# Three more gate pairs by seven products in an attention + GEGLU kernel on one Trainium2 core

## The chip, the core and the metric

The kernel runs on one core of one Trainium2 chip. The metric is the device time of one execution in microseconds (us), as the median of several runs. The engines of the core work side by side and meet through semaphores: TensorE (PE) multiplies, VectorE (DVE) and ScalarE (ACT) work element by element and are the ones that read PE's results out of PSUM here, GpSimd (POOL) works element by element on SBUF, and SyncE (SP) issues most DMAs. PSUM has eight banks, numbered 0 to 7, each of 128 partitions by 512 f32 numbers.

## What is computed

```python
# q, k, v: (8 batches, 8 heads, 576, 64); heads 0-3 use a plain window of 32, heads 4-7 a window of 32 with step 4
scores = scale * q @ k.T                      # masked to the window
attn   = softmax(scores) @ v
x      = attn.transpose(0, 2, 1, 3).reshape(4608, 512)
g      = x @ w_gate                           # (512, 1536)
val    = x @ w_val                            # (512, 1536)
out    = (gelu(g) * val) @ w_out              # (1536, 512) -> (4608, 512)
```

## The kernel before

**Chunks.** The 4608 tokens are worked off in nine chunks of 512 (c = 0 to 8). A chunk has a gate phase and an out phase. In the gate phase the 12 blocks nb = 0 to 11 of 128 hidden columns are made: four matmuls of 128x512 for the gate and four for the value (L623), the gelu on ACT (`g`, L1012), and the product of both on DVE into `u_all` (`u`, L1017, which reads the value from its PSUM bank). In the out phase `u_all` is multiplied by `w_out` (L805). Attention of the next batch stands between the matmuls of the out phase, in chunks 0 to 6; chunks 7 and 8 have none.

**Seven products in the out phase.** From chunk 1 on, the out phase takes a 2x2 split of `u` (two blocks of a pair j = 0 to 5, times two halves of the tokens) and of `w_out`, and makes the product with seven block products in place of eight, in the order 1, 7, 6, 4, 5, 2, 3 over two banks (`ORDER`, `products`). Product 7 needs `ux[j, 0]` of all six pairs, product 6 needs `ux[j, 2]` of all, product 3 a half of `u_all` that is written anew. These sums are DVE's: `u_sums(j, 0)` (word `kj@0`, L766), then `kj@1@n` for n pairs at once (L771), then `kj@2@n` (L773). `part_out` (word `q`) takes parts of the result out of the banks; `q0` is a snapshot on DVE in chunks 1 to 6 (L843, into `vdiag`), after product 1 and before product 6 adds to the same bank.

**Seven products in the gate phase.** For some pairs of blocks (`IN_SEVEN`; pair j holds nb = 2j and 2j + 1) the gate phase does the same with `x` and the weights. A word `fj@product@bank` issues one product: four matmuls of 128x256 (L688), gate and value side by side in one bank. The order is 1, 2, 6, 7, 5, 4, 3, over two banks A and B by turns: 1, 6, 5, 3 go to A, and 2, 7, 4 to B. After products 1, 6 and 7 ACT copies the bank to a snapshot (`quarter_out`, L702; `vdiag`, `turned` or `stage`), after 2, 5 and 4 DVE adds a snapshot to the bank (L709, into a tile `quarter`), and product 3 is copied by ACT (L707). The next product in a bank has to wait for that read. Each of the four quarters then has its gelu on ACT (L717, 256 wide) and its product on DVE (L726, which reads two SBUF tiles). The four sums of `x` that the products use are POOL's in chunks 6 to 8 (`x_sums`, L670); those of chunk 8 are written over those of chunk 7, and their word `x8` stands in chunk 7's out phase. The sums of the weights (`gate_sums`, L655, words `hj@part`) are made once: for pair 1 by DVE in chunk 2, for pair 2 by POOL in chunk 6.

**What sets the order.** Each engine runs its instructions in the order of the program. That order is written out by hand: `gate_words` and `out_words` give strings of words, and a number in them issues so many of the phase's 128x512 or 128x256 matmuls. `BLOCKS[c]` says, for the pairs by seven products, how many product words follow each half block (`slots`), which words stand behind them (`after`), and which stand at the end. `gate_banks` gives each ordinary block its two banks. Before, pair 1 is made by seven products in chunks 3 to 8, and pair 2 in chunks 7 and 8.

Of the kernel before, what the change touches and what calls it, by code (L numbers as in the profile page):

```python
# [21 lines left out]
def kernel(  # L22
# [21 lines left out]
    NCH = NT // CH  # L44
# [42 lines left out]
    stage = const.tile([P, 3840], F32, tag="stage")  # L87
# [7 lines left out]
    snap = [vdiag.bitcast(F32)[:, DM * i : DM * i + DM] for i in range(2)] + [turned[:, 0:DM]]  # L95
# [70 lines left out]
    tiles = {}  # L166
# [458 lines left out]
    def parts_of(order):  # L625
        return [(kc, i == 0, i == len(order) - 1) for i, kc in enumerate(order)]

    ONE = ((1, (1, 4)),)
    IN_PLACES = {c: ONE if c < 7 else ONE + ((2, (2, 3)),) for c in range(3, NCH)}
    IN_SEVEN = {c: [j for j, _ in IN_PLACES[c]] for c in IN_PLACES}  # L630
    sums_at = {1: 0, 2: 2 * CH, 3: 3 * CH}
    free_pool = range(6, NCH)

    def sums_of(j, s):

        return x_all[:, s, sums_at[j] : sums_at[j] + CH].rearrange("p (m k n) -> p m k n", m=2, k=2)

    def quarters(j, m):

        i = next(i for i, (_, end) in enumerate(WC) if 2 * j * P < end)  # L640
        w = (wg_t, wv_t)[m][i][:, :, 2 * j * P - WC[i][0] : 2 * j * P - WC[i][0] + 2 * P]
        return [[w[:, 2 * k : 2 * k + 2, P * n : P * n + P] for k in range(2)] for n in range(2)]

    def gate_sums(j, part):

        for m in range(2):
            (a11, a12), (a21, a22) = quarters(j, m)
            s1, s2, s3, s4 = (sums_of(j, s)[:, m] for s in range(4))
# [6 lines left out]
            (nc.vector if j == 1 else nc.gpsimd).tensor_tensor(out_, first, other, op)  # L655
# [41 lines left out]
    def quarter_out(c, j, kind, bank):  # L697

        src, kept = ps[:, bank, :], {1: 0, 6: 1, 7: 2}.get(kind)
        saved = snap if bank in (1, 4) else [stage[:, DM * i : DM * i + DM] for i in range(3)]  # L700
        if kept is not None:
            nc.scalar.copy(saved[kept], src)  # L702
            return
        n = tiles["quarters"] = tiles.get("quarters", 0) + 1
        t = nrm.tile([P, S], F32, tag=("rb", "lg", "rb", "lg", "rb")[n % 5], bufs=(3, 2, 3, 2, 3)[n % 5], name="quarter")[:, 0:DM]
        if kind == 3:
            nc.scalar.copy(t, src)  # L707
        else:
            nc.vector.tensor_tensor(t, src, saved[{2: 0, 4: 1, 5: 2}[kind]], ALU.add)  # L709
        nb, half = 2 * j + (kind in (4, 5)), int(kind in (3, 5))  # L710
        tiles.setdefault("ready", []).append((nb, half, t))
# [238 lines left out]
    def gate_banks(c, nb):  # L950

        if c == 0:
            return ((4, 5), (6, 7))[nb] if nb < 2 else ((0, 1), (2, 3))[nb % 2]
        if c in IN_SEVEN:
            if nb in (1, 11):
                return (1, 4)
            if c > 6:
                return (5, 6) if nb % 2 else (0, 7)
            return (4, 1) if nb == 9 else (0, 7)
        return ((0, 7), (1, 6) if c == 1 else (1, 4))[nb % 2]  # L960

    SEVEN = range(1, NCH)
# [1 line left out]
    def gate_list(c):  # L964
# [28 lines left out]
    def run_program(c, words, mms, banks):  # L993
# [3 lines left out]
        for word in words.split():  # L997
# [12 lines left out]
            elif kind == "g":  # L1010
                g = ffn.tile([P, CH], F16, tag="g")
                nc.scalar.activation(g, ps[:, gate_banks(c, args[0])[0], :], AF.Gelu)  # L1012
                tiles["g", args[0]] = g
            elif kind == "u":
# [47 lines left out]
    def gate_words(c):  # L1062
# [35 lines left out]
    one = (  # L1098
        [0, 1, 1, 0, 1, 1, 0, 1, 1, 1, 0, 0, 0, 0, 0],
        "||k0@0||k2@0||||k3@0|k3@1@2|U k3@2@2|U|U k4@0|k1@0|k1@1@2",  # L1100
    )
    late = "|".join(w + h for w, h in zip(one[1].split("|"), [""] * 11 + [" h2@0", " h2@1", " h2@2", " h2@3"]))
    two = (
        [0, 2, 2, 2, 2, 2, 2, 2, 0, 0, 0],
        "k0@0||||k3@0|||U|U k4@0|U k1@0 k2@0|k2@1@3",
    )
    BLOCKS = {c: (*one, "", "") for c in range(3, 6)}
    BLOCKS[6] = (one[0], late, "", "")
    BLOCKS[7] = BLOCKS[8] = (*two, "", "u11 k5@0 k5@1@3 k2@2@3 k5@2@3")

    def seven_words(c):

        pairs = IN_PLACES[c]
        orders = [[f"f{j}@{product}@{banks[n % 2]}" for n, product in enumerate((1, 2, 6, 7, 5, 4, 3))] for j, banks in pairs]
        pairs = [j for j, _ in pairs]
        groups = orders[0] if len(pairs) == 1 else [w for both in zip(*orders[:2]) for w in both]
# [12 lines left out]
    def out_words(c):

        if c == 0:
            return (
                "V1 F2 S6@4+S7@6 1 E P6 11 P7 1 M6 S4@4+S5@6 M7 1 P4 6 P5 M4 2 D6@40+D7@60 l6 l7 M5 r6 r7 6 w2@0 4 w1@0 4 "
                "w0@0 H2 N6@50+N7@20 D4@52+D5@22 X6 l5 X7 l4 r4 r5 10 N4@20+N5@40 X4 X5 2 e3@0"
            )
        if c > 6:
            return "12 q0@1 x8 12 q1@1 12 q2@1 12 q3@0 12 q4@0 12 q5@0 12 q6@1" if c < NCH - 1 else "L"
        i, j, k, l = (NHP * (c + 1) + n for n in range(NHP))
        v0, v1 = (" v0", " v1") if 2 < c < 6 else ("", "")
        late = "k1@2@2 " if c in IN_SEVEN else ""  # L1140
# [14 lines left out]
    }  # L1155
# [38 lines left out]
```

## Time and profile before

| | |
|---|---|
| median of 3 runs | 315.9 us (315.34 to 315.94) |
| the profiled execution | 316.73 us, of which span 315.0 us |
| busy in the span | DVE 227.7 us, ACT 179.5 us, POOL 104.4 us |
| granted PE clock | 1.00 |
| gate phase and out phase of chunk 7 | 252.92 to 272.93 us and 272.93 to 282.22 us |
| gate phase and out phase of chunk 8 | 282.22 to 302.14 us and from 302.14 us on |

A row of the timeline has the start, the time to the end of the last instruction, the engine, the line, the operation, what is written and read with its shape, and the count; in brackets stands idle time before it and what ended it. Matmuls are pipelined: each is shown from its issue to its modelled end, so rows overlap, and the step from one start to the next is the time that it costs PE. DVE and ACT overlap the start of one instruction with the end of the one before in the same way.

### The profile page before, as it was taken

The numbers are of one execution on the slowest core, as the hardware profiler recorded it, in microseconds if no ns is written. First come the engines' busy times: TensorE is split into PE (matmuls) and PEld (weight loads), VectorE is DVE, ScalarE is ACT, GpSimd is POOL, SyncE is SP. The second block draws the span as 40 slices with busy tenths as digits, with TensorE's granted clock in tenths as the row PEclk, the third lists the DMA queues.
The fourth block names the chain that finished last, engine by engine and source line by source line (L and its number), as shares of the span: only waits on it lengthen the run. The fifth ranks groups of instructions, "written<-read, shape, count | busy, mean of one in ns | idle before, by whom it ended". The sixth has DMA issues, their size and how long they took to land.

```text
span 315.0 us, 8745 instructions
## 1 busy us (share of the span) xinstructions
PE 308.0 (98%) x3585; PEld 193.2 (61%) x3585; DVE 227.7 (72%) x408; ACT 179.5 (57%) x295; POOL 104.4 (33%) x154
## 2 busy tenths in 40 slices
PE   7999999999999999999999999999999999999995
PEld 4854545446854486557755775568556856686674
DVE  6863656698866798698858886797568757944772
ACT  2673476535763387547754675567556765524740
POOL 8784703312367160233126031504730052300000
PEclk9999999999999999999999999999999999999999
DMA  8999998898699998889889667965200220021004
GB/s 188 186 197 206 206 198 150 241 207 194 152 281 180 198 221 157 237 202 212 184 220 251 156 180 174 230 156 146 67 0 4 69 69 0 2 99 36 0 0 135
DMA packets 110791, 47.16 MB, mean 150 GB/s; under 512 B 83616, under 2 KB 110240, under 8 KB 110752
## 3 DMA queue, kind: packets, MB, share of 16 engines
q1 hardware_dynamic: 97248, 38.29, 53.9%
q0 software_dynamic: 12944, 7.67, 19.1%
q10 hardware_dynamic: 560, 0.66, 0.8%
q8 instruction: 28, 0.46, 0.7%
q14 instruction: 11, 0.09, 0.1%
HBM read 37.75 MB, written 9.44 MB: 150 GB/s over the span
## 4 chain that ended last, share of the span: by engine, by line
PE 88%; DVE 5%; DMA 4%; POOL 1%; issue 1%; ACT 0%; DVEq 0%
PE ps L623 49%; PE ps L805 21%; PE ps L688 8%; PE ps L458 6%; PE ps L730 3%; DMA wg<-in_moe_w_gate_dram 2%; DMA xT<-in_q_dram 2%; DVE u_all L1017 1%; DVE ux L766 1%; DVE ux L771 1%; DVE P L493 1%; DVE vdiag L843 1%; DVE u_all L726 0%; POOL xT L182 0%; PE ps L378 0%
## 5 line engine op out<-in xcount | busy, mean ns | idle before, releaser
L1012 ACT ACTIVATE g<-ps 128x512 f16<-128x512 f32 x92 | 54.8, 597 | 78.8 <-PE ps L623 78.7
L1017 DVE SCALAR_TENSOR_TENSOR u_all<-g,ps 128x512 f16<-128x512 f16 x92 | 63.0, 685 | 49.9 <-PE ps L623 33.3
L623 PE MATMUL ps<-xT,wv 128*128 128x512 f16 x368 | 95.8, 379 | 0.0
L623 PE MATMUL ps<-xT,wg 128*128 128x512 f16 x368 | 95.0, 379 | 0.2
L623 PEld LDWEIGHTS <-wg 128*128 128x128 f16 x368 | 35.8, 98 | 38.7 <-DMA wg<-in_moe_w_gate_dram 0.2
L623 PEld LDWEIGHTS <-wv 128*128 128x128 f16 x368 | 36.0, 98 | 37.0 <-DMA wv<-in_moe_w_val_dram 0.4
L805 PEld LDWEIGHTS <-u_all 128*128 128x128 f16 x390 | 36.8, 98 | 7.1 <-issue 1.1
L805 PE MATMUL ps<-wx,ux 128*128 128x256 f16 x288 | 35.5, 273 | 0.6 <-DVE vdiag L843 0.5
L805 PE MATMUL ps<-wo,u_all 128*128 128x256 f16 (+1 forms) x294 | 35.2, 271 | 0.0
L254 POOL CAST v<-stage 128x1152 f16<-128x1152 f32 x11 | 13.0, 1177 | 64.4 <-DMA stage<-in_v_dram 48.2
L217 POOL CAST s<-stage 128x640 f16<-128x640 f32 x24 | 17.7, 767 | 44.5 <-DMA stage<-in_q_dram 31.1
L614 DVE TENSOR_TENSOR xT<-ps,rb 128x576 f16<-128x576 f32 x32 | 29.1, 940 | 4.7 <-PE ps L458 3.2
L488 ACT ACTIVATE P<-ps 128x832 f16<-128x832 f32 (+1 forms) x32 | 25.3, 834 | 12.1 <-PE ps L458 12.0
L805 PEld LDWEIGHTS <-ux 128*128 128x128 f16 x288 | 27.6, 98 | 4.9 <-issue 1.0
L670 POOL TENSOR_TENSOR xT<-xT 128x512 f16<-128x512 f16 x12 | 13.9, 1182 | 33.0 <-DVE xT L614 25.4
L766 DVE TENSOR_TENSOR ux<-u_all 128x512 f16<-128x512 f16 x48 | 22.4, 478 | 0.8
L585 ACT ACTIVATE lg<-ps 128x576 f32<-128x576 f32 x30 | 18.8, 656 | 6.6 <-PE ps L458 3.6
L229 POOL CAST s<-stage 128x512 f16<-128x512 f32 x24 | 16.2, 700 | 8.8 <-DMA stage<-in_q_dram 8.1
L591 ACT ACTIVATE rb<-lg 128x576 f32<-128x576 f32 x30 | 19.0, 687 | 0.1
L688 PE MATMUL ps<-xT 128*128 128x256 f16 x128 | 17.9, 273 | 0.0
L726 DVE SCALAR_TENSOR_TENSOR u_all<-g,quarter 128x256 f16<-128x256 f16 x32 | 15.8, 497 | 1.8 <-ACT g L717 1.8
L688 PEld LDWEIGHTS <-xT 128*128 128x128 f16 x128 | 12.5, 98 | 6.6
(113 smaller groups left out, 358.2 us busy)
## 6 DMA issues: line engine op xcount, KB each, us to landing
out_dram<-part SPq DMA_DIRECT2D x30, 256.0 KB, 2.8
stage<-in_v_dram SPq DMA_DIRECT2D x28, 144.0 KB, 3.5
stage<-in_q_dram SPq DMA_DIRECT2D x24, 128.0 KB, 3.5
stage<-in_k_dram SPq DMA_DIRECT2D x24, 128.0 KB, 3.0
stage<-in_q_dram SPq DMA_DIRECT2D x6, 512.0 KB, 4.9
stage<-in_k_dram SPq DMA_DIRECT2D x6, 512.0 KB, 5.5
stage<-in_v_dram SPq DMA_DIRECT2D x20, 128.0 KB, 3.4
wo<-in_moe_w_out_dram POOLq DMA_DIRECT2D x3, 512.0 KB, 15.7
```

The costliest lines, as they stand in the source:

```text
L217: nc.gpsimd.tensor_copy(s16[:, 1280 * t + 640 * g : 1280 * t + 640 * g + 640].rearrange("p (k c) -> p k c", k=5), st_of(i).rearrange("p (k ...
L458: nc.tensor.matmul(o[cols], lhs[rows], rhs[rows], start=st, stop=end, skip_group_check=True)
L488: nc.scalar.activation(pt[:, 0 : src.shape[1]], src, AF.Exp, bias=0.0, scale=scale)
L585: nc.scalar.activation(lg, psf[:, c0 : c0 + S], AF.Ln)
L591: nc.scalar.activation(rb, tiles.pop(("lg", n)), AF.Exp, scale=-1.0)
L614: nc.vector.tensor_tensor(dst, num, rb, ALU.mult)
L623: nc.tensor.matmul(ps[:, bank, :], w[:, kc, ns], xT[kc][:, tok], start=first, stop=end)
L688: nc.tensor.matmul(ps[:, bank, 2 * P * m : 2 * P * m + 2 * P], left[:, k], right[:, k], start=first and m == 0 and k == 0, stop=k == 1, sk ...
L766: nc.vector.tensor_tensor(ux[:, j, 0:2], k0, u_all[:, 2 * j : 2 * j + 2, hi], ALU.subtract)
L805: lambda o=o, s=s[:, P * p : P * p + P], t=t[:, c0:c1], st=st, end=end: nc.tensor.matmul(o, s, t, start=st, stop=end, skip_group_check=True)
L1012: nc.scalar.activation(g, ps[:, gate_banks(c, args[0])[0], :], AF.Gelu)
L1017: nc.vector.scalar_tensor_tensor(u_all[:, nb, :], tiles.pop(("g", nb)), -USCALE if c in SEVEN and nb % 2 else USCALE, val, ALU.mult, ALU.mult)
```

## The change

Chunk 6 makes pairs 1 and 2 by seven products, one pair behind the other in the banks 1 and 4. Chunks 7 and 8 make pairs 1, 2 and 3 (a, b and c in `in_turn`) on the banks 1 and 2, 6 and 3, 4 and 5. Six products stand together behind block 1, then three behind each half block. Blocks 8, 9 and 10 all use the banks 0 and 7, block 11 the banks 3 and 5. In chunks 7 and 8 product 3 is no longer copied: gelu and product read it from its bank. The sums of pair 2's weights move from POOL in chunk 6 to DVE in chunk 5; POOL makes those of pair 3 in chunk 6. In the out phases of chunks 1 to 6 the snapshot `q0` moves ahead of `k5@1`, and in chunk 6 `k3@2` covers pairs 2 and 3 late.

```diff
-    ONE = ((1, (1, 4)),)
-    IN_PLACES = {c: ONE if c < 7 else ONE + ((2, (2, 3)),) for c in range(3, NCH)}
-    IN_SEVEN = {c: [j for j, _ in IN_PLACES[c]] for c in IN_PLACES}
+    IN_PLACES = {c: {1: (1, 4)} for c in range(3, 6)}
+    IN_PLACES[6] = {1: (1, 4), 2: (4, 1)}
+    IN_PLACES[7] = IN_PLACES[8] = {1: (1, 2), 2: (6, 3), 3: (4, 5)}
+    IN_SEVEN = {c: list(IN_PLACES[c]) for c in IN_PLACES}
...
-            (nc.vector if j == 1 else nc.gpsimd).tensor_tensor(out_, first, other, op)
+            (nc.gpsimd if j == 3 else nc.vector).tensor_tensor(out_, first, other, op)
...
+        if kind == 3 and c > 6:
+            tiles.setdefault("ready", []).append((2 * j, 1, src))
+            return
...
-            if nb in (1, 11):
-                return (1, 4)
-            if c > 6:
-                return (5, 6) if nb % 2 else (0, 7)
-            return (4, 1) if nb == 9 else (0, 7)
+            if nb == 11:
+                return (1, 4) if c < 7 else (3, 5)
+            return (1, 4) if nb == 1 else (4, 1) if nb == 9 and c < 6 else (0, 7)
...
     two = (
-        [0, 2, 2, 2, 2, 2, 2, 2, 0, 0, 0],
-        "k0@0||||k3@0|||U|U k4@0|U k1@0 k2@0|k2@1@3",
+        [0, 2, 2, 2, 2, 2, 2, 1, 1, 0, 0],
+        "k0@0||||k3@0|h3@0||k1@0 k1@1@2|U k4@0|U h3@1|U h3@2 k2@0",
     )
...
+    early = ["", " h2@0", "", " h2@1", "", " h2@2", " h2@3"]
+    BLOCKS[5] = (one[0], "|".join(w + h for w, h in zip(one[1].split("|"), early + [""] * 8)), "", "")
...
-    BLOCKS[7] = BLOCKS[8] = (*two, "", "u11 k5@0 k5@1@3 k2@2@3 k5@2@3")
+    three = ([6, 3, 3, 3, 3, 3, 0], "k0@0||||k4@0|U k1@0|U")
...
+    BLOCKS[6] = (*two, "h3@3 k3@1@2", "")
+    BLOCKS[7] = BLOCKS[8] = (*three, "U k2@0 k3@0", "u11 k5@0 k3@1@4 k5@1@2 k3@2@4 k5@2@2")
+    in_turn = "a1 b1 a2 a6 b2 a7 a5 b6 c1 a4 b7 c2 a3 b5 c6 b4 c7 c5 b3 c4 c3"
...
-            f"E P{i} P{j} 1 u11 k5@0 k5@1@2 11 q0@0 M{i} M{j}{v0} {late}k5@2@2 12 q1@1 8 "
+            f"E P{i} P{j} 1 u11 k5@0 11 q0@0 k5@1@2 M{i} M{j}{v0} {late}k5@2@2 12 q1@1 8 "
```

The first place is DVE's queue at the end of chunk 3's gate phase, before the change: the last block's product, the last pair's sums, the snapshot `vdiag`, and the masks of the attention tiles `P`.

```order
L1017 SCALAR_TENSOR_TENSOR u_all<-g,ps 128x512
L766 TENSOR_TENSOR ux<-u_all 128x512
L771 TENSOR_TENSOR ux<-u_all,ux 128x2x256
L843 TENSOR_SCALAR vdiag<-ps 128x512
L493 TENSOR_TENSOR P_2480<-P_2480,two_p 128x832
```

And with the change (L847 is the snapshot, L775 the sum that stood ahead of it):

```order
L1019 SCALAR_TENSOR_TENSOR u_all<-g,ps 128x512
L770 TENSOR_TENSOR ux<-u_all 128x512
L847 TENSOR_SCALAR vdiag<-ps 128x512
L775 TENSOR_TENSOR ux<-u_all,ux 128x2x256
L493 TENSOR_TENSOR P_2480<-P_2480,two_p 128x832
```

The snapshot has moved ahead of one sum; nothing else has moved there.

The second place is ACT's queue at the start of chunk 7's gate phase, before the change: the load of the gelu table, the gelus of blocks 0 to 2, the first snapshots of pairs 1 and 2 and the gelu of block 3.

```order
L1059 ACT_TABLE_LOAD
L1012 ACTIVATE g<-ps 128x512 x3
L702 COPY vdiag<-ps 128x512
L702 COPY stage<-ps 128x512
L1012 ACTIVATE g<-ps 128x512
```

And with the change:

```order
L1061 ACT_TABLE_LOAD
L1014 ACTIVATE g<-ps 128x512 x2
L703 COPY vdiag<-ps 128x512
L703 COPY stage<-ps 128x512
L703 COPY vdiag<-ps 128x512
L721 ACTIVATE g<-quarter 128x256
```

The gelu of the third block is gone from there: the products of a pair now follow block 1 directly.

The third place is DVE's queue in the last third of chunk 7's gate phase. Before, from the last read of a bank for a quarter (L709) on: quarters' products (L726), blocks 9, 10 and 11 (L1017), and the sums `ux`.

```order
L709 TENSOR_TENSOR quarter<-ps,stage 128x512
L726 SCALAR_TENSOR_TENSOR u_all<-g,quarter 128x256 x3
L1017 SCALAR_TENSOR_TENSOR u_all<-g,ps 128x512
L726 SCALAR_TENSOR_TENSOR u_all<-g,quarter 128x256
L766 TENSOR_TENSOR ux<-u_all 128x512
L726 SCALAR_TENSOR_TENSOR u_all<-g,quarter 128x256
L766 TENSOR_TENSOR ux<-u_all 128x512 x2
L1017 SCALAR_TENSOR_TENSOR u_all<-g,ps 128x512
```

With the change, from block 9 (L1019) to block 10 (the last row), where three reads for quarters (L713) still stand:

```order
L1019 SCALAR_TENSOR_TENSOR u_all<-g,ps 128x512
L730 SCALAR_TENSOR_TENSOR u_all<-g,ps 128x256
L713 TENSOR_TENSOR quarter<-ps,stage 128x512
L730 SCALAR_TENSOR_TENSOR u_all<-g,quarter 128x256
L713 TENSOR_TENSOR quarter<-ps,stage 128x512
L770 TENSOR_TENSOR ux<-u_all 128x512
L730 SCALAR_TENSOR_TENSOR u_all<-g,quarter 128x256
L713 TENSOR_TENSOR quarter<-ps,stage 128x512
L730 SCALAR_TENSOR_TENSOR u_all<-g,quarter 128x256
L730 SCALAR_TENSOR_TENSOR u_all<-g,ps 128x256
L770 TENSOR_TENSOR ux<-u_all 128x512
L1019 SCALAR_TENSOR_TENSOR u_all<-g,ps 128x512
```

Behind these twelve rows come two more quarters' products, two sums, block 11, the last pair's first sum, and `k3@1@4`, a sum over four pairs in one instruction. Before, the reads for quarters were over when the last sums began; now they stand among them.

More of the change, by code (lines that the diff above doesn't have):

```diff
@@ L699, in quarter_out @@
         src, kept = ps[:, bank, :], {1: 0, 6: 1, 7: 2}.get(kind)
-        saved = snap if bank in (1, 4) else [stage[:, DM * i : DM * i + DM] for i in range(3)]
+        saved = snap if j == 1 else [stage[:, DM * i : DM * i + DM] for i in range(3 * j - 6, 3 * j - 3)]
         if kept is not None:
             nc.scalar.copy(saved[kept], src)
+            return
+        if kind == 3 and c > 6:
+            tiles.setdefault("ready", []).append((2 * j, 1, src))
             return
@@ L1101 @@
     )
-    late = "|".join(w + h for w, h in zip(one[1].split("|"), [""] * 11 + [" h2@0", " h2@1", " h2@2", " h2@3"]))
+    early = ["", " h2@0", "", " h2@1", "", " h2@2", " h2@3"]
     two = (
-        [0, 2, 2, 2, 2, 2, 2, 2, 0, 0, 0],
-        "k0@0||||k3@0|||U|U k4@0|U k1@0 k2@0|k2@1@3",
-    )
-    BLOCKS = {c: (*one, "", "") for c in range(3, 6)}
-    BLOCKS[6] = (one[0], late, "", "")
-    BLOCKS[7] = BLOCKS[8] = (*two, "", "u11 k5@0 k5@1@3 k2@2@3 k5@2@3")
-    def seven_words(c):
[L1113 to L1116, printed above, removed]
+        [0, 2, 2, 2, 2, 2, 2, 1, 1, 0, 0],
+        "k0@0||||k3@0|h3@0||k1@0 k1@1@2|U k4@0|U h3@1|U h3@2 k2@0",
+    )
+    three = ([6, 3, 3, 3, 3, 3, 0], "k0@0||||k4@0|U k1@0|U")
+    BLOCKS = {c: (*one, "", "") for c in range(3, 5)}
+    BLOCKS[5] = (one[0], "|".join(w + h for w, h in zip(one[1].split("|"), early + [""] * 8)), "", "")
+    BLOCKS[6] = (*two, "h3@3 k3@1@2", "")
+    BLOCKS[7] = BLOCKS[8] = (*three, "U k2@0 k3@0", "u11 k5@0 k3@1@4 k5@1@2 k3@2@4 k5@2@2")
+    in_turn = "a1 b1 a2 a6 b2 a7 a5 b6 c1 a4 b7 c2 a3 b5 c6 b4 c7 c5 b3 c4 c3"
+    def seven_words(c):
+        places = IN_PLACES[c]
+        order = (1, 2, 6, 7, 5, 4, 3)
+        turns = [(j, product) for j in places for product in order]
+        if len(places) == 3:
+            turns = [("_abc".index(w[0]), int(w[1])) for w in in_turn.split()]
+        groups = [f"f{j}@{product}@{places[j][order.index(product) % 2]}" for j, product in turns]
+        pairs = list(places)
         direct = [nb for nb in range(2, NNB - 1) if nb // 2 not in pairs]
@@ L1139, in out_words @@
         v0, v1 = (" v0", " v1") if 2 < c < 6 else ("", "")
-        late = "k1@2@2 " if c in IN_SEVEN else ""
+        late = "" if c < 3 else "k1@2@2 " if c < 6 else "k1@2@2 k3@2@2 "
         after = f"S{l + 1}@12+S{l + 2}@15" if 1 < c < 6 else ""
         return (
-            f"E P{i} P{j} 1 u11 k5@0 k5@1@2 11 q0@0 M{i} M{j}{v0} {late}k5@2@2 12 q1@1 8 "
+            f"E P{i} P{j} 1 u11 k5@0 11 q0@0 k5@1@2 M{i} M{j}{v0} {late}k5@2@2 12 q1@1 8 "
             f"S{k}@1+S{l}@4 D{i}@11+D{j}@41 P{k} P{l} 4 q2@0 M{k} M{l}{v1} 12 l{i} l{j} r{i} r{j} q3@0 "
```

## The prediction

> **What bounds the kernel now.** I read the page first (busy shares, then the chain), then the windows of chunks 7 and 8, then the timeline of the places that the change touches.
>
> ```profile
> span 315.0 us, 8745 instructions
> PE 308.0 (98%) x3585; PEld 193.2 (61%) x3585; DVE 227.7 (72%) x408; ACT 179.5 (57%) x295; POOL 104.4 (33%) x154
> PE 88%; DVE 5%; DMA 4%; POOL 1%; issue 1%; ACT 0%; DVEq 0%
> 252.92:272.93 20.01, 20.01 (x123) 11.74 (x121) 15.12 (x27) 13.29 (x26) 8.27 (x7) 1.00 0.08 26
> 282.22:302.14 19.92, 19.92 (x122) 11.73 (x120) 13.00 (x27) 11.90 (x25) 0.00 (x0) 1.00 0.08 27
> ```
>
> PE is busy 98% of the span and carries 88% of the chain. In the gate phases of chunks 7 and 8 (the windows; columns PE, PEld, DVE, ACT, POOL) it has no gap at all. So PE columns that are saved are time saved, as long as DVE, the next engine at 15.12 of 20.01 us in chunk 7, still empties banks and delivers sums in time. That is the question.
>
> **What the change saves on PE.** PE's step is read where nothing waits, in chunk 8:
>
> ```profile
> 290.01 1.04 PE L688 MATMUL ps<-xT 128*128 128x256 f16 x8
> 290.88 1.03 PE L623 MATMUL ps<-xT,wv 128*128 128x512 f16 x4
> 291.74 1.04 PE L688 MATMUL ps<-xT 128*128 128x256 f16 x8
> ```
>
> Eight matmuls of 128x256 take 0.87 us from start to start, four of 128x512 take 0.86: 0.109 and 0.216 each. A pair made the ordinary way is 16 x 0.216 = 3.46, by seven products 28 x 0.109 = 3.05. Saved are 0.40 us a pair, and three more pairs (one each in chunks 6, 7, 8) give **-1.2**.
>
> **The snapshot ahead of the second sum.** Chunk 3, then chunk 4:
>
> ```profile
> 143.23 0.76 DVE L766 TENSOR_TENSOR ux<-u_all 128x512 f16<-128x512 f16 x1
> 144.02 0.86 DVE L771 TENSOR_TENSOR ux<-u_all,ux 128x512 f16<-128x512 f16 x1
> 144.81 0.68 DVE L843 TENSOR_SCALAR vdiag<-ps 128x512 f32<-128x512 f32 x1
> 143.55 1.47 PE L805 MATMUL ps<-wx,ux 128*128 128x256 f16 x12
> 145.54 1.03 PE L805 MATMUL ps<-wx,ux 128*128 128x256 f16 x8 [0.52 <-DVE vdiag L843]
> 177.55 0.68 DVE L843 TENSOR_SCALAR vdiag<-ps 128x512 f32<-128x512 f32 x1
> 176.71 2.61 PE L805 MATMUL ps<-wx,ux 128*128 128x256 f16 x20
> ```
>
> In chunk 3 product 7 began at 143.55, so product 6 was due 12 x 0.109 later, at 144.86, and began at 145.54, 0.05 after the snapshot's end: 0.68 lost. With the sum behind it the snapshot starts at 143.9 and ends at 144.6, in time. In chunk 4 twenty matmuls end after 2.61 us where 19 steps and one whole instruction (0.38 less 0.11, as eight take 1.04) make 2.34: 0.27 lost, and gone too. The sum moved back is needed only by product 6's last two pairs, 0.9 us later. But in chunk 3 the masks behind it still have to pass POOL's casts, and PE, now earlier, meets them. Bounds 0 and -0.95; I take **-0.6**.
>
> **Start of chunk 7.** Product a1 goes to bank 1, where block 1's gate lies until its gelu has read it.
>
> ```profile
> 256.22 0.60 ACT L1012 ACTIVATE g<-ps 128x512 f16<-128x512 f32 x1 [0.60 <-PE ps L623]
> 256.45 0.38 PE L623 MATMUL ps<-xT,wg 128*128 128x512 f16 x1
> ```
>
> The second row is the first matmul behind block 1, an ordinary one in bank 0. In its place now stands a1, which must wait for 256.82 and the 0.05 seen above: 0.42 of PE standing. Then a7 wants bank 2 after DVE's add on a2, with two products (0.87) between; the add takes 0.68, the hand-overs around it 0.27 and 0.05 (rows below): 0.1. Together **+0.5** (bounds 0.4 and 0.7). In chunk 8 block 1's gate comes four matmuls earlier, and this is nothing.
>
> **End of chunk 7.** This is the large term. The instructions' steps on DVE, and what POOL's subtractions for chunk 8 do to them:
>
> ```profile
> 258.19 1.03 PE L623 MATMUL ps<-xT,wv 128*128 128x512 f16 x4
> 259.32 0.69 DVE L1017 SCALAR_TENSOR_TENSOR u_all<-g,ps 128x512 f16<-128x512 f16 x1 [1.12 <-PE ps L623]
> 259.93 0.68 DVE L709 TENSOR_TENSOR quarter<-ps,vdiag 128x512 f32<-128x512 f32 x1
> 260.53 0.68 DVE L709 TENSOR_TENSOR quarter<-ps,stage 128x512 f32<-128x512 f32 x1
> 265.38 4.98 POOL L670 TENSOR_TENSOR xT<-xT 128x512 f16<-128x512 f16 x4 [7.46 <-PE ps L688]
> 266.62 1.15 POOL L670 TENSOR_TENSOR xT<-xT 128x512 f16<-128x512 f16 x1
> 267.73 2.63 POOL L670 TENSOR_TENSOR xT<-xT 128x512 f16<-128x512 f16 x2
> 267.48 0.57 DVE L726 SCALAR_TENSOR_TENSOR u_all<-g,quarter 128x256 f16<-128x256 f16 x1
> 268.57 2.41 DVE L726 SCALAR_TENSOR_TENSOR u_all<-g,quarter 128x256 f16<-128x256 f16 x3
> 271.50 0.41 DVE L726 SCALAR_TENSOR_TENSOR u_all<-g,quarter 128x256 f16<-128x256 f16 x1
> 271.84 0.41 DVE L766 TENSOR_TENSOR ux<-u_all 128x512 f16<-128x512 f16 x1
> 272.17 0.41 DVE L726 SCALAR_TENSOR_TENSOR u_all<-g,quarter 128x256 f16<-128x256 f16 x1
> 273.78 0.55 DVE L771 TENSOR_TENSOR ux<-u_all,ux 128x768 f16<-128x768 f16 x1
> L726 DVE SCALAR_TENSOR_TENSOR u_all<-g,quarter x32: 411/419/1378, 133.2 to 300.5; 128x256 f16<-128x256 f16 x32
> ```
>
> PE's last matmul ends 0.17 after its issue (1.03 less 0.86), and DVE starts 0.10 later (259.32). An instruction that reads a bank steps by 0.60, a quarter's product or a 512-wide sum by 0.34. Those have both inputs in SBUF, and while POOL ran (265.38 to 270.36) the same product took 0.57 and then 2.41 for three, its longest 1.38 against a median of 0.42. The bank reads in the same stretch kept their 0.68. The 0.57 one ended at 268.05, 0.28 after POOL's second subtraction (until 267.77): of its 0.41 it had used 0.13. POOL in turn was held: with 1.02 of its 1.15 still to run after each DVE instruction, the last two end at 268.05 + 1.02 + 0.28 + 1.02 = 270.37, as the row has it (267.73 + 2.63). So the two take turns, each for its whole length.
>
> Now the queue. Let T be when c5, the 18th of the 21 products, has left PE's issue. Behind it PE issues blocks 10 and 11 (16 x 0.216), b3, c4, c3 (12 x 0.109), and the out phase's products 1 and 7 (24 x 0.109): product 6 is due at T + 7.4. It needs `k3@1@4`. On DVE that instruction stands behind block 9's product, which starts at T - 1.04 (its value matmuls leave PE three products, 1.31, earlier, and end and hand over 0.27 later). From there come six bank reads at 0.60 and twelve short ones at 0.34, 0.11 of waits on own results (the sum of 144.02 began 0.03 after the end it needed, where bank reads overlap by 0.08), and the sum over four pairs at 0.69 (0.55 for three pairs in the last row but one, 0.42 for two): 8.5, so T + 7.5. **Without POOL DVE arrives just in time**, 0.1 late.
>
> But POOL's four subtractions begin as c5 ends, at T + 0.2, as they began in the trace when the last product 5 had ended. Walked by the turns above: DVE's product at T + 0.51 waits for POOL's first to end (T + 1.35) and ends at T + 1.63; the sum at T + 2.15 waits for the second and ends at T + 2.93; the product at 2.85 waits for the third, until T + 4.23; the one at 4.75 for the fourth, until T + 5.53. The next instruction starts at T + 5.45, where it would stand at T + 3.07 undisturbed: 2.4 lost, and product 6 is late by **+2.5**, part of it earlier, at c3, block 11's value and product 7, which wait in the same queue. Bounds: 0.1 if POOL runs clear of it, 4.2 if each of the four turns costs a whole 1.02; the 1.46 that the before lost in its own 5 us (0.57 + 2.41 for four, against 4 x 0.34 and 0.15 of overlap) lies between. I take my walk. The before loses almost nothing here, as its last bank reads are over by then: 24 matmuls took 2.90 in chunk 7 against 2.78 in chunk 8, **-0.1** of an old wait that the new one contains.
>
> ```profile
> 274.24 2.90 PE L805 MATMUL ps<-wx,ux 128*128 128x256 f16 x24
> 303.45 2.78 PE L805 MATMUL ps<-wx,ux 128*128 128x256 f16 x24
> ```
>
> The Trainium skill ("SBUF — State Buffer", section "Who interferes with whom") speaks against the change here: a DVE instruction with two SBUF inputs and a GpSimd instruction that reads SBUF share a port pair under an exclusive lock, and the later one blocks fully. The 1.38 and the 0.28 agree. By a proportional slowdown, say the 1.46 again, the term would be 1.6 and not 2.5.
>
> **The rest.** Chunk 8 has the same queue without POOL (0.00 in its window): some 0.1, and DVE's waits for gelus, which chunk 7 hides in its backlog; bounds 0 and 0.7, I take **+0.4**. In chunk 6 DVE has about two us more (three bank reads and four short ones for two bank reads), with six products on one bank pair by turns: bounds 0 and 0.6, **+0.2**. In chunk 5 eight weight sums come to DVE,
>
> ```profile
> L655 DVE TENSOR_TENSOR xT<-wg x2: 283/284/284, 97.4 to 104.4; 128x256 f16<-128x256 f16 x2
> ```
>
> at 0.28 each, 0.20 in step, 1.6 in all, beside POOL's casts of batch 7: bounds 0 and 0.8, **+0.3**. POOL's own sums in chunk 6 are as many as before. Product 3 without its copy takes work from ACT, which has slack (13.29 of 20.01), and costs or gains nothing; its quarter's product then reads a bank, which POOL doesn't disturb, and the banks it keeps are wanted only a phase later. No DMA moves.
>
> **Sum.** -1.2 - 0.6 + 0.5 + 2.5 - 0.1 + 0.4 + 0.2 + 0.3 = **+2.0**. On the profiled execution (316.73, span 315.0) that is 318.7; the median of the runs is 0.8 lower, 315.9, so I forecast **317.9**.
>
> **Rivals.** *POOL runs clear of DVE* (not slower): if DVE's short instructions fall between POOL's, or DVE is ahead, the 2.5 shrinks to 0.1 and the sum to -0.4: 315.5. It decides at the end of chunk 7, at whether `k3@1@4` ends by T + 7.4. For it speaks that the queue fits without POOL; against it that the four subtractions take 5 us and that four two-input instructions stand in just that stretch. *PE is bound by its columns alone* (faster): every wait hidden, -1.2 - 0.95 = -2.1: 313.8. Against it stands the wait of a1, which no queue can hide. *The backlog costs more* (slower): all turns at their full price and chunks 5, 6 and 8 at their upper bounds, about +4.9: 320.8; with chunks 5, 6 and 8 alone at theirs, +3.2: 319.1.
>
> **How the numbers follow.** Forecast 0.74, from about +0.8 to +3.2, 316.7 to 319.1; POOL clear 0.12; columns alone 0.04; more 0.10. A difference of 0.2% (0.6 us) is about what a measurement of this kernel can tell from none. The POOL rival's time lies within it or just below: 0.06 faster, 0.06 same. So faster is 0.06 + 0.04 = 0.10, same 0.06, slower 0.74 + 0.10 = 0.84. The range for 8 in 10 runs from 316.0, toward the POOL rival, to 319.4, into the heavier one.
>
> **What would show it.** Right: in chunk 7 a PE wait of 0.4 on ACT's gelu ahead of the first L689 row; four POOL rows (L671) of 1.15 to 1.35 from the end of the 18th product on, with DVE rows L730 or L770 of 0.8 to 1.4 between them; PE idle on DVE in front of c3, block 11's value and the out phase's products 7 and 6, 2.5 us in all; in chunk 8 only some tenths; no wait on the snapshot L847 in chunks 3 and 4. Wrong: chunk 7's two phases no longer than 28.9 us (29.3 before, less 0.4), or DVE's L730 at 0.42 throughout.

## The result, and the profile after

The changed kernel takes 318.99 us (median of 6 runs, 318.08 to 319.57) against 316.03 of the kernel before in the runs beside it (315.34 to 317.02): a ratio of **1.0076, interval 1.0052 to 1.01**, so slower. The profiled execution took 319.11 us, its span 317.3 against 315.0.

Busy shares and the chain, from the page of the kernel after:

```profile
span 317.3 us, 8850 instructions
PE 307.6 (97%) x3621; PEld 195.9 (62%) x3621; DVE 234.4 (74%) x431; ACT 184.4 (58%) x307; POOL 104.6 (33%) x154
PE 85%; DVE 8%; POOL 2%; DMA 2%; issue 1%; ACT 0%
```

PE is busy 0.4 us less than before and the span is 2.3 us longer: DVE's share of the chain grew from 5% to 8%. The same window as in the prediction shows where, from the start of chunk 7's gate phase to that of chunk 8 (columns: length, then PE, PEld, DVE, ACT, POOL, clock, DMA share, GB/s):

```profile
252.67:284.54 31.87, 30.08 (x219) 20.56 (x217) 23.81 (x42) 16.33 (x32) 8.34 (x7) 1.00 0.10 33
```

The two phases took 29.30 us before (252.92 to 282.22), with PE busy throughout; now 31.87, with PE idle for 1.8 by its rows and for 3.0 by its steps (a row runs on to the modelled end, which covers part of a wait). The timeline of PE says what it waits for: first the masks in chunks 1 and 2, the out phase of chunk 3, a stall at 187 us, block 9 in chunk 6, then the start of chunk 7, its end, and chunk 8:

```profile
80.68 0.55 PE L458 MATMUL ps<-P,ones 64*64 64x96 f16 x22 [0.24 <-DVE P L493]
...
114.38 0.55 PE L458 MATMUL ps<-P,ones 64*64 64x96 f16 x22 [0.37 <-DVE P L493]
...
144.16 2.35 PE L809 MATMUL ps<-wx,ux 128*128 128x256 f16 x20
...
186.03 0.54 PE L458 MATMUL ps<-q 64*64 64x96 f16 x35
187.42 0.19 PE L458 MATMUL ps<-q 64*64 64x64 f16 x1 [0.85 <-issue]
...
256.62 0.38 PE L689 MATMUL ps<-xT,wg 128*128 128x256 f16 x2 [0.25 <-ACT g L1014]
...
268.09 1.03 PE L623 MATMUL ps<-xT,wg 128*128 128x512 f16 x4
...
270.42 0.60 PE L689 MATMUL ps<-xT 128*128 128x256 f16 x4 [0.43 <-DVE quarter L713]
...
273.01 1.02 PE L623 MATMUL ps<-xT,wv 128*128 128x512 f16 x4 [0.27 <-DVE quarter L713]
...
275.98 0.95 PE L809 MATMUL ps<-wx,ux 128*128 128x256 f16 x6 [0.17 <-DVE ux L770]
277.37 0.39 PE L809 MATMUL ps<-wx,ux 128*128 128x256 f16 x2 [0.45 <-DVE ux L770]
277.98 1.48 PE L809 MATMUL ps<-wx,ux 128*128 128x256 f16 x12 [0.21 <-DVE ux L775]
...
284.54 1.03 PE L623 MATMUL ps<-xT,wg 128*128 128x512 f16 x4
...
304.22 1.47 PE L809 MATMUL ps<-wo,u_all 128*128 128x256 f16 x12
```

Each bracket understates a wait by 0.17, the tail of the matmul before it. Counted from start to start, less the 0.109 or 0.216 of each matmul, the end of chunk 7 loses 0.60 ahead of c3 (270.42), 0.43 ahead of block 11's value (273.01), 0.34, 0.11 and 0.61 inside product 7, and 0.37 ahead of product 6 (277.98): **2.46 us**. In chunk 3, twenty matmuls of products 7 and 6 run in 2.35, as they should; the wait on the snapshot is gone. Chunk 8's gate phase, 284.54 to 304.22, is 19.68 long against 19.92 before.

DVE's timeline at the same place, from block 9's product on:

```profile
266.98 0.69 DVE L1019 SCALAR_TENSOR_TENSOR u_all<-g,ps 128x512 f16<-128x512 f16 x1 [0.28 <-PE ps L623]
267.58 0.41 DVE L730 SCALAR_TENSOR_TENSOR u_all<-g,ps 128x256 f16<-128x256 f16 x1
267.91 0.68 DVE L713 TENSOR_TENSOR quarter<-ps,stage 128x512 f32<-128x512 f32 x1
268.51 1.25 DVE L730 SCALAR_TENSOR_TENSOR u_all<-g,quarter 128x256 f16<-128x256 f16 x1
269.69 0.68 DVE L713 TENSOR_TENSOR quarter<-ps,stage 128x512 f32<-128x512 f32 x1
270.29 0.78 DVE L770 TENSOR_TENSOR ux<-u_all 128x512 f16<-128x512 f16 x1
270.99 1.37 DVE L730 SCALAR_TENSOR_TENSOR u_all<-g,quarter 128x256 f16<-128x256 f16 x1
272.28 0.68 DVE L713 TENSOR_TENSOR quarter<-ps,stage 128x512 f32<-128x512 f32 x1
272.88 0.77 DVE L730 SCALAR_TENSOR_TENSOR u_all<-g,quarter 128x256 f16<-128x256 f16 x1
273.58 0.41 DVE L730 SCALAR_TENSOR_TENSOR u_all<-g,ps 128x256 f16<-128x256 f16 x1
...
277.23 1.02 DVE L775 TENSOR_TENSOR ux<-u_all,ux 128x1024 f16<-128x1024 f16 x2
```

And POOL's, whose four subtractions of `x8` fill 268.33 to 273.37:

```profile
268.33 5.04 POOL L671 TENSOR_TENSOR xT<-xT 128x512 f16<-128x512 f16 x4 [10.64 <-PE ps L689]
```

Exactly the four instructions with two SBUF inputs that start in that stretch are long, 1.25, 0.78, 1.37 and 0.77 where undisturbed ones take 0.41 or 0.42; the reads of a bank between them (269.69, 272.28) keep 0.68. All products of line L730 that read a tile `quarter`, with minimum, median and maximum in ns:

```profile
L730 DVE SCALAR_TENSOR_TENSOR u_all<-g,quarter x38: 410/417/1370, 133.8 to 303.7; 128x256 f16<-128x256 f16 x38
```

The longest of the whole kernel is the one at 270.99; half of the 38 take 0.417 or less.

### The profile page after: what moved, and what is told of

Read it like the earlier page. It is cut to its first block, busy times and chain, and to the rows that moved or that the text cites. A ratio compares the mean times of both kernels' runs of the same rounds, so it can differ in the third digit from the quotient of the medians.

```text
span 317.3 us, 8850 instructions
## 1 busy us (share of the span) xinstructions
PE 307.6 (97%) x3621; PEld 195.9 (62%) x3621; DVE 234.4 (74%) x431; ACT 184.4 (58%) x307; POOL 104.6 (33%) x154
## 4 chain that ended last, share of the span: by engine, by line
PE 85%; DVE 8%; POOL 2%; DMA 2%; issue 1%; ACT 0%
PE ps L623 45%; PE ps L809 21%; PE ps L689 9%; PE ps L458 6%; PE ps L734 3%; DMA wg<-in_moe_w_gate_dram 2%; DVE u_all L730 2%; DVE u_all L1019 1%; DVE P L493 1%; DVE ux L770 1%; DVE quarter L713 1%; POOL xT L182 1%; POOL v L313 1%; DVE vdiag L847 0%; DVE ux L775 0%
## 5 line engine op out<-in xcount | busy, mean ns | idle before, releaser
L1019 DVE SCALAR_TENSOR_TENSOR u_all<-g,ps 128x512 f16<-128x512 f16 x86 | 58.7, 684 | 44.3 <-PE ps L623 29.6
L623 PE MATMUL ps<-xT,wv 128*128 128x512 f16 x344 | 89.7, 379 | 0.3 <-DVE quarter L713 0.3
L623 PE MATMUL ps<-xT,wg 128*128 128x512 f16 x344 | 88.8, 379 | 0.1
L1014 ACT ACTIVATE g<-ps 128x512 f16<-128x512 f32 x86 | 51.2, 597 | 64.3 <-PE ps L623 64.1
L623 PEld LDWEIGHTS <-wv 128*128 128x128 f16 x344 | 33.5, 98 | 35.4 <-issue 1.0
L623 PEld LDWEIGHTS <-wg 128*128 128x128 f16 x344 | 33.4, 98 | 35.5 <-DMA wg<-in_moe_w_gate_dram 0.2
L217 POOL CAST s<-stage 128x640 f16<-128x640 f32 x24 | 17.9, 776 | 42.8 <-DMA stage<-in_q_dram 30.7
L689 PE MATMUL ps<-xT 128*128 128x256 f16 x176 | 24.8, 273 | 0.4 <-DVE quarter L713 0.4
L689 PEld LDWEIGHTS <-xT 128*128 128x128 f16 x176 | 16.9, 98 | 8.1 <-issue 0.6
L770 DVE TENSOR_TENSOR ux<-u_all 128x512 f16<-128x512 f16 x48 | 20.9, 443 | 0.8
L730 DVE SCALAR_TENSOR_TENSOR u_all<-g,quarter 128x256 f16<-128x256 f16 x38 | 19.4, 510 | 0.7 <-ACT g L721 0.7
```

The source lines that it names most:

```text
L623: nc.tensor.matmul(ps[:, bank, :], w[:, kc, ns], xT[kc][:, tok], start=first, stop=end)
L689: nc.tensor.matmul(ps[:, bank, 2 * P * m : 2 * P * m + 2 * P], left[:, k], right[:, k], start=first and m == 0 and k == 0, stop=k == 1, sk ...
L730: nc.vector.scalar_tensor_tensor(dst, g, by, t[:, 2 * P : 4 * P], ALU.mult, ALU.mult)
L770: nc.vector.tensor_tensor(ux[:, j, 0:2], k0, u_all[:, 2 * j : 2 * j + 2, hi], ALU.subtract)
L1019: nc.vector.scalar_tensor_tensor(u_all[:, nb, :], tiles.pop(("g", nb)), -USCALE if c in SEVEN and nb % 2 else USCALE, val, ALU.mult, ALU.mult)
```

## The experiments

The theory: the 2.46 us at the end of chunk 7 come from POOL's four subtractions, which stop DVE's two-input instructions in turns while PE waits on DVE's queue. The rivals: DVE's queue has simply become too long there (three pairs' quarters, then a sum over four pairs at the end), or the turns are an old cost that the kernel before paid as well. A second theory, on 0.4 us, is the bank of the first product.

Each ratio is taken against the kernel before in runs beside the version's own. Its median there was 316.72 us for `x8` on DVE, its control, the swapped banks and the three edits together, and 316.38 for the other four, where it was 316.03 beside the change. So versions are compared by their ratios, not by their times.

**The `x8` subtractions on DVE.** One number takes them from POOL; DVE makes them after `k3@2@4`.

```diff
-    free_pool = range(6, NCH)
+    free_pool = range(6, NCH - 1)
```

> The changed kernel with chunk 8's four x subtractions on DVE, where they stand behind the last u sum of chunk 7, in place of POOL. Theory (POOL and DVE take turns at the end of chunk 7): PE's waits there, 2.5 us in the trace of the change (c3, block 11's value, products 7 and 6), shrink to 0.1 to 0.5, DVE's L730 products stay at 0.42, and the time falls by 2.2 to 2.6 us, to about 316.5, 1.001 to 1.003 of before. Rival (DVE simply has too much to do for three pairs): four more DVE instructions of 0.42 make it no better, 319 to 320.

Measured: 315.95 us (315.39 to 318.09, 12 runs), ratio 0.9982 (0.9961 to 1.0003), below the 1.001 to 1.003 that was expected. DVE's timeline at the same place:

```profile
267.85 0.42 DVE L730 SCALAR_TENSOR_TENSOR u_all<-g,quarter 128x256 f16<-128x256 f16 x1
268.18 0.68 DVE L713 TENSOR_TENSOR quarter<-ps,stage 128x512 f32<-128x512 f32 x1
268.78 0.42 DVE L770 TENSOR_TENSOR ux<-u_all 128x512 f16<-128x512 f16 x1
269.12 0.42 DVE L730 SCALAR_TENSOR_TENSOR u_all<-g,quarter 128x256 f16<-128x256 f16 x1
...
275.92 1.62 DVE L671 TENSOR_TENSOR xT<-xT 128x512 f16<-128x512 f16 x4
```

And PE's, from the out phase's product 1 on:

```profile
272.19 1.47 PE L809 MATMUL ps<-wo,u_all 128*128 128x256 f16 x12
273.50 2.78 PE L809 MATMUL ps<-wx,ux 128*128 128x256 f16 x24
```

All six waits are gone: the 24 matmuls of products 7 and 6 take the 2.78 us that they take undisturbed. DVE's queue up to the sum that product 6 needs is as long as in the change (the 1.62 us of subtractions stand behind it), and PE waits for nothing in it. So a queue that is too long by itself falls as a cause. The span is 314.1, 3.2 shorter; 2.46 of that are these waits, and 0.65 the stall at 187 us, which is 0.36 in this run and 1.01 in that of the change and was no part of the expectation (more on it at the end of the next section).

**The same edit on the kernel before**, as a control.

> The kernel before with chunk 8's x subtractions on DVE, as in e1: the control. Theory: POOL's subtractions cost PE 0.1 us there, since the reads of banks are over when they run, so -0.1, within 0.1% of before, although DVE's products of 0.57 to 1.38 us go. Rival (the subtractions on POOL cost a fixed price wherever they stand): -2 us, as in e1.

Measured: 315.9 us (315.49 to 318.13, 12 runs), ratio 0.9984 (0.9966 to 1.0002). The 0.11 at product 7 is gone; a gain beyond that isn't resolved. So the turns were not an old cost of this size: the subtractions ran in the kernel before too, beside instructions that nobody waited for.

**The subtractions once more, in chunk 8.** Here POOL repeats them at the same point of the last chunk, which has the same queue on DVE and no POOL work in the change. No later instruction uses what they write.

```diff
-            return "12 q0@1 x8 12 q1@1 ... 12 q6@1" if c < NCH - 1 else "L"
+            return "12 q0@1 x8 12 q1@1 ... 12 q6@1" if c < NCH - 1 else "x8 L"
```

> The changed kernel in which POOL makes chunk 8's four x subtractions once more, into the same places, as soon as chunk 8's products have read them: the suspected cost added at the end of chunk 8, where POOL had nothing to do; nothing reads the result. Theory (two-input DVE instructions and POOL's reads take turns): PE waits at the end of chunk 8 for 2.5 us more, DVE's L730 and L770 of 0.8 to 1.4 us appear there, +2.4 to +2.6 us, about 321.5. Rival (chunk 7's waits come from DVE's load, POOL is a bystander): the same 319.0.

Measured: 321.4 us (320.99 to 321.8, 4 runs), ratio 1.0147 (1.0097 to 1.0197), 0.7% above the change. PE's timeline in chunk 8:

```profile
301.19 0.60 PE L689 MATMUL ps<-xT 128*128 128x256 f16 x4 [0.43 <-DVE quarter L713]
...
303.78 1.02 PE L623 MATMUL ps<-xT,wv 128*128 128x512 f16 x4 [0.27 <-DVE quarter L713]
...
305.44 1.36 PE L809 MATMUL ps<-wo,u_all 128*128 128x256 f16 x11 [0.53 <-ACT g L1014]
307.67 2.78 PE L809 MATMUL ps<-wx,ux 128*128 128x256 f16 x24 [0.88 <-DVE u_all L1019]
```

The waits ahead of c3 and block 11's value are those of chunk 7, 0.60 and 0.43. Then come 0.69 ahead of the second matmul of product 1 and 1.04 ahead of product 7: 2.76 in all, where the change has 0.22. DVE's held instructions are those of chunk 7 again, 1.25, 0.77, 1.37 and 0.77 (at 299.28, 301.06, 301.76 and 303.65). The mechanism could be put where it was wanted, at the price of chunk 7, though the waits behind it fall on other instructions: product 7 here waits for DVE's read of block 11's value (L1019), which lies in bank 5.

**POOL busy at that point, but not reading.** Four memsets of the same four pieces in place of the repeated subtractions; no later instruction uses them.

```diff
+            elif kind == "Z":
+                for s in (1, 0, 2, 3):
+                    nc.gpsimd.memset(x_all[:, s, CH : 2 * CH], 0.0)
...
-            return "12 q0@1 x8 12 q1@1 ... 12 q6@1" if c < NCH - 1 else "L"
+            return "12 q0@1 x8 12 q1@1 ... 12 q6@1" if c < NCH - 1 else "Z L"
```

> As e5, but POOL sets the four 128x512 pieces of the x sums to zero at that point in place of subtracting: it writes SBUF and reads none; nothing reads the result. Theory (the turns are over reads): DVE keeps 0.42, no change, 319.0. Rival (any POOL instruction on SBUF blocks DVE's two-input ones): +0.5 to +2.5 us, by how long the memsets run.

Measured: 318.06 us (317.77 to 319.57, 10 runs), ratio 1.0051 (1.0027 to 1.0075), no slower than the change. POOL's timeline in chunk 8:

```profile
298.54 1.45 POOL L1045 MEMSET xT<- 128x512 f16 x3 [26.31 <-PE ps L689]
300.28 0.52 POOL L1045 MEMSET xT<- 128x512 f16 x1 [0.28 <-PE ps L689]
```

And DVE's beside it:

```profile
298.74 0.42 DVE L730 SCALAR_TENSOR_TENSOR u_all<-g,quarter 128x256 f16<-128x256 f16 x1
299.07 0.69 DVE L713 TENSOR_TENSOR quarter<-ps,stage 128x512 f32<-128x512 f32 x1
299.68 0.42 DVE L770 TENSOR_TENSOR ux<-u_all 128x512 f16<-128x512 f16 x1
```

The product at 298.74 lies wholly within the row of three memsets (298.54 to 299.99, 0.48 each) and takes its 0.42, and so does the sum at 299.68, which starts within it; PE's waits in chunk 8 stay at the 0.34 of the change. The turns are over reads of SBUF, then, not over POOL being busy or writing. One input is enough: where POOL casts, in the change for instance in the row of two casts (L217) from 135.96 to 137.54, DVE's sum at 136.99 (L775, two inputs in SBUF) takes 0.82 in place of 0.42 and ends 0.27 after the second. The Trainium skill ("SBUF — State Buffer", section "Who interferes with whom") says that a DVE instruction with two SBUF inputs contends with a GpSimd instruction that reads SBUF and not with one that only writes it; the traces agree (0.82 and 0.42).

**The first pair's banks swapped.** Product a1 then goes to bank 2 and a2 to bank 1.

```diff
-    IN_PLACES[7] = IN_PLACES[8] = {1: (1, 2), 2: (6, 3), 3: (4, 5)}
+    IN_PLACES[7] = IN_PLACES[8] = {1: (2, 1), 2: (6, 3), 3: (4, 5)}
```

> The changed kernel with pair 1's two banks of chunks 7 and 8 exchanged (2 and 1), so that a1 no longer goes to the bank that block 1's gelu reads. Theory: PE's wait of 0.42 us ahead of a1 goes, nothing else, since POOL's subtractions and DVE's queue at the chunk's end move with PE: -0.4, to about 318.6. Rival (the end of chunk 7 is set by DVE's queue alone): the 0.4 comes back as a longer wait at the end, and the time stays at 319.0.

Measured: 317.99 us (317.27 to 319.02, 10 runs), ratio 1.0051 (1.0033 to 1.0069). PE's timeline at the start of chunk 7, the last two matmuls of block 1 and then a1 (its gate side, its value side):

```profile
254.98 0.59 PE L623 MATMUL ps<-xT,wv 128*128 128x512 f16 x2
255.41 0.38 PE L689 MATMUL ps<-xT,wg 128*128 128x256 f16 x2
255.63 0.38 PE L689 MATMUL ps<-xT,wv 128*128 128x256 f16 x2
```

a1 starts 0.43 after the row ahead of it, the step of its two matmuls: the 0.42 is gone, and the six waits at the end of the chunk are unchanged (0.60, 0.43, 0.34, 0.11, 0.61, 0.37), so the 0.42 did not come back there, against the rival. A gate that is to be read late and a product that wants its bank at once had been put on the same bank. In the medians the gain is not resolved: the two intervals overlap.

**Three edits together.** Subtractions on DVE, banks swapped, and in chunks 1 and 2 the old order of snapshot and sum, to see whether their mask waits come from the move.

```diff
+        first = "11 q0@0 k5@1@2" if c > 2 else "k5@1@2 11 q0@0"
...
-            f"E P{i} P{j} 1 u11 k5@0 11 q0@0 k5@1@2 M{i} M{j}{v0} {late}k5@2@2 12 q1@1 8 "
+            f"E P{i} P{j} 1 u11 k5@0 {first} M{i} M{j}{v0} {late}k5@2@2 12 q1@1 8 "
```

> The changed kernel with the subtractions on DVE, pair 1's banks exchanged, and the snapshot ahead of the second sum in chunks 3 to 6 only. Theory: the three gains add up, 2.5 + 0.4 + 0.4 for the masks of chunk 2 (whose wait grew from 0.11 to 0.53 us): 319.0 - 3.3 = 315.7, 0.997 to 1.000 of before. Rival (the edits overlap): 316.2 or more.

Measured: 315.58 us (314.94 to 317.08, 12 runs), ratio 0.997 (0.9953 to 0.9987), the lower end of the 0.997 to 1.000 that was expected. PE's timeline in chunk 2, at product 6:

```profile
112.60 1.03 PE L809 MATMUL ps<-wx,ux 128*128 128x256 f16 x8 [0.43 <-DVE vdiag L847]
```

The mask wait of chunk 1 is down to 0.13 and that of chunk 2 is gone, and a wait of 0.60 on the snapshot stands in chunk 2; one of 0.31 stands in chunk 3, where the snapshot is ahead of the sum. That the old order took the mask waits away is not shown by this: `x8` twice and the memsets have the change's order there, and mask waits of 0.13 and less (table below).

**The snapshot's move alone**, on the kernel before.

```diff
-            f"E P{i} P{j} 1 u11 k5@0 k5@1@2 11 q0@0 M{i} M{j}{v0} {late}k5@2@2 12 q1@1 8 "
+            f"E P{i} P{j} 1 u11 k5@0 11 q0@0 k5@1@2 M{i} M{j}{v0} {late}k5@2@2 12 q1@1 8 "
```

> The kernel before with one edit of the change: the snapshot ahead of the second sum in chunks 1 to 6. Theory: the snapshot's waits of chunks 3 and 4 (0.68 and 0.26 in the trace of before) go, the mask's wait of chunk 2 grows from 0.11 to 0.53: -0.5 us, 0.998 of before. Rival (the waits move from the snapshot to the masks, and their size is a matter of when POOL's casts fall): 0.999 to 1.001, with mask waits in the trace in place of snapshot waits.

Measured: 316.18 us (315.12 to 317.01, 12 runs), ratio 0.9981 (0.996 to 1.0003). PE's timeline in chunk 3:

```profile
144.28 2.35 PE L805 MATMUL ps<-wx,ux 128*128 128x256 f16 x20
...
147.36 0.57 PE L458 MATMUL ps<-P,ones 64*64 64x96 f16 x26 [0.23 <-DVE P L493]
```

The wait on the snapshot is gone, and the masks, 3 us later, cost 0.39 in its place (0.23 and the tail); chunk 1 has 0.42 there. The gain is at most a part of the 0.95, and this measurement does not tell it from none. The execution also has two stalls that the profile puts down to nothing, 0.76 at 118.74 and 0.58 at 187 us.

**What is left, put together.** From the change: subtractions on DVE, banks swapped, block 11 on the banks 3 and 1, in chunk 6 a sum (`k1@1@2`) one half block later so that block 9 comes sooner, and in chunks 1 to 6 the masks ahead of the sum as well.

```diff
-    IN_PLACES[7] = IN_PLACES[8] = {1: (1, 2), 2: (6, 3), 3: (4, 5)}
+    IN_PLACES[7] = IN_PLACES[8] = {1: (2, 1), 2: (6, 3), 3: (4, 5)}
-    free_pool = range(6, NCH)
+    free_pool = range(6, NCH - 1)
-                return (1, 4) if c < 7 else (3, 5)
+                return (1, 4) if c < 7 else (3, 1)
-        "k0@0||||k3@0|h3@0||k1@0 k1@1@2|U k4@0|U h3@1|U h3@2 k2@0",
+        "k0@0||||k3@0|h3@0||k1@0|U k1@1@2 k4@0|U h3@1|U h3@2 k2@0",
-            f"E P{i} P{j} 1 u11 k5@0 11 q0@0 k5@1@2 M{i} M{j}{v0} {late}k5@2@2 12 q1@1 8 "
+            f"E P{i} P{j} 1 u11 k5@0 11 q0@0 M{i} M{j}{v0} k5@1@2 {late}k5@2@2 12 q1@1 8 "
```

> e1's and e2's edits, and three more: in chunks 1 to 6 the masks too stand ahead of the second sum, block 11 of chunks 7 and 8 uses the banks 3 and 1 (product 7 of chunk 8 goes to bank 5), and chunk 6's sum k1@1 stands one half block later. Theory: PE's waits left in e1 go at five places, 0.45 for masks, 0.42 on a1, 0.17 in chunk 6 and 0.2 in chunk 8: 1.2 us less than e1, 0.994 to 0.996 of before. Rival (the sum moved back is then late for product 6): as e1 or slower, 0.998 or more.

Measured: 314.9 us (314.09 to 316.39, 12 runs), ratio **0.9951 (0.9929 to 0.9973)**: faster than the kernel before and than the change, and within the 0.994 to 0.996 that was expected. Its page:

```profile
span 312.8 us, 8849 instructions
PE 94%; DMA 2%; ACT 1%; DVE 1%; POOL 1%; issue 0%
```

PE carries 94% of the chain, and of waits over 0.1 us from 60 us on three are left: 0.12 on DVE's read of a bank at 173.3, and 0.15 and 0.14 on a2's bank in chunks 7 and 8.

PE's waits of the profiled executions side by side, from 60 us on, counted as above (us; below 0.1 left out):

| | chunks 1 to 5: masks + snapshot + all else, the stall at 187 us above all | chunk 6 | start of 7 | end of 7 | chunk 8 | span |
|---|---|---|---|---|---|---|
| before | 0.46 + 0.95 + 0.65 | 0 | 0 | 0.11 | 0 | 315.0 |
| the change | 0.96 + 0 + 1.01 | 0.17 | 0.56 | 2.46 | 0.34 | 317.3 |
| banks swapped | 1.12 + 0 + 0.11 | 0.17 | 0.15 | 2.46 | 0.34 | 316.1 |
| `x8` on DVE | 0.72 + 0 + 0.36 | 0.17 | 0.56 | 0 | 0.36 | 314.1 |
| `x8` on DVE, kernel before | 0 + 0.62 + 0 | 0 | 0 | 0 | 0 | 313.8 |
| three edits | 0.13 + 0.91 + 0.48 | 0.17 | 0.14 | 0 | 0.36 | 313.8 |
| `x8` twice | 0.13 + 0 + 1.12 | 0.17 | 0.56 | 2.45 | 2.88 | 319.2 |
| memsets | 0 + 0.12 + 0.22 | 0.17 | 0.56 | 2.46 | 0.34 | 316.1 |
| snapshot's move on the kernel before | 0.82 + 0 + 1.34 | 0 | 0 | 0.11 | 0 | 315.2 |
| five edits | 0 + 0 + 0.12 | 0 | 0.15 | 0 | 0.14 | 312.8 |

The columns of chunks 6 to 8 repeat to 0.01 or 0.02 us wherever the code is the same. The first one doesn't: the five kernels with the same code up to there (the change, banks swapped, `x8` on DVE, `x8` twice, memsets) have 0.3 to 2.0 us in it.

## Why the prediction was right

The forecast was 317.9 us, in a range to 319.4, slower; the median was 318.99 and the profiled difference +2.3 of span where the sum said +2.0. By its own steps:

**End of chunk 7, +2.5: 2.46, and for the reason given.** The walk by turns put times on each instruction, counted from T, the moment when c5 has left PE's issue (268.09 above):

| | predicted | measured |
|---|---|---|
| POOL's first subtraction starts | T + 0.2 | 0.24 |
| first product held until | T + 1.63 | 1.67 |
| sum held until | T + 2.93 | 2.98 |
| second product held until | T + 4.23 | 4.27 |
| third product held until | T + 5.53 | 5.56 |
| next instruction starts | T + 5.45 | 5.49 |

That the term is POOL's was shown by taking it away on the spot (2.46 to 0), by making it a second time in chunk 8 (2.76 there), and by a POOL that is busy without reading (nothing). A proportional slowdown, 1.6, would have been too little.

**Columns, -1.2: borne out.** Chunk 8's gate phase is 19.68 with 0.12 of waits in it, 19.56 against 19.92 before: 0.36 for a pair that was to save 0.40. That of chunk 6 (220.86 to 240.95, before 220.88 to 241.20) is 19.92 without its 0.17 against 20.32, which is 0.40; that of chunk 7 (252.67 to 273.87) is 19.52 without its waits against 19.93, which is 0.41 (0.08 ahead of its second block taken off in both). The rival in which POOL runs clear of DVE was put on the chip by the first experiment: 0.9982 of before, which is 315.5 on the 316.03 of the result, where it had been priced at 315.5.

**Start of chunk 7, +0.5: 0.42 on the gelu and 0.15 on a2's bank.** The swap removed the first and left the second.

**Snapshot, -0.6: about -0.45 in the profiled execution, and in the medians not shown.** Both waits went, 0.95 together. But chunks 1 and 2, which the prediction left out, had no wait on the snapshot to lose, and their masks, behind the moved snapshot on DVE, cost 0.96 there instead of 0.46. Even the -0.45 is the difference of two single executions: over the five kernels with the change's code up to there, masks and snapshot together cost 0.12 to 1.12 (table), and in the two with the code of before 1.41 and 0.62. What sets the masks' waits is not shown. The move alone gives 0.9981 (0.996 to 1.0003). With the masks ahead of the sum too, in the last version, neither wait was seen.

**The rest.** Chunk 8: +0.4 predicted, 0.34 found, not for the gelus but at a2's bank (0.12) and at product 7 (0.22), which goes to bank 5, where block 11's value still had to be read; that the size fits is luck. Chunk 6: +0.2 predicted, 0.17, at one place, block 9's value. Chunk 5: +0.3 predicted and nothing found, so DVE's eight weight sums were covered.

**What no step had.** The stall at 187.4 us is 0.36 longer than before. Chunk 5's 0.3 that didn't come about makes up for it in the sum, and that is luck. The profile names no wait for the stall, but the trace's DMA records have a queue of the kind "instruction" (q8, packets of 16 KB) whose times fit it. In all ten profiles the last attention matmul, the one behind the stall, starts 1.29 to 1.51 us after the end of the q8 packet ahead of it, and the stall is long where that packet starts late: 1.12 where it starts 1.18 us before the matmul is due (`x8` twice), 1.01 at 1.33 (the change), 0.65 at 1.64 (before), and 0.17 or less from 2.4 us on. The stall of 0.76 at 118.74 in the snapshot's version ends 1.30 after such a packet too. So PE probably waits there for its instructions, and whether the packet comes late in an execution is chance as far as these runs go; none of them varied it, so this cause is not shown.

The medians differ by 2.96, the profiled executions by 2.38, since that of before lay 0.70 above the median of the runs beside it and that of the change 0.12. The interval of the ratio is 1.6 to 3.2 us, which has room for the sum's +2.0.

## What to carry to other kernels

An engine that is far from busy can still set the end: POOL has 33% of this span, and four of its instructions, none of which anybody waited for, cost PE 2.46 us by stopping DVE where PE had come to wait on DVE. When work is moved, ask of each side engine not only when its result is needed, but beside which instructions of another engine it will now run, and put such work where the other engine has slack; here DVE itself made the four subtractions in 1.62 us for POOL's 5.04. When a read is moved ahead, ask as well what it is now in front of, and in the chunks where nothing was waiting.

## What the runs showed of the hardware

- DVE's instructions with two SBUF inputs and POOL's that read SBUF take turns, each for its whole length, to the point where a walk by turns hits every end within 0.05 us. The median of 0.42 becomes 1.25 and 1.37 where about 1.0 and 1.1 us of a subtraction are still to run, and POOL's four take 5.04 instead of 4.6. POOL's casts, with one input, hold DVE in the same way (0.82 in place of 0.42 at 136.99).
- Not held are POOL's memsets (DVE 0.42 beside them) and DVE instructions with one input in PSUM (0.68 for the reads at 269.69 and 272.28, as elsewhere).
- PE's stall ahead of the last attention matmul at 187 us is 0.1 to 1.12 us over the five kernels with the change's code there and 0.65 and 0 in the two with the code of before. It is shown as "issue", with no engine behind it; PE's clock was granted at 1.00. The matmul follows 1.29 to 1.51 us behind a 16 KB packet of the instruction queue in all ten profiles, which makes a late load of instructions the likely cause, not a shown one. Differences of up to 1 us between single profiled executions of this kernel can't be read without taking it out first.
